# Chunk rows by engine copies, two halves of the first MLP weight, and a new order in a sparse attention and MLP kernel

## The chip, the cores and the metric

The kernel runs on one core of a Trainium2 chip. TensorE (PE in the profile, PEld for its weight loads), VectorE (DVE), ScalarE (ACT) and GpSimd (POOL) work side by side, each through its own list of instructions in order; SyncE (SP) issues most DMAs, GpSimd those that change the type, ScalarE a few. The metric is the device time of one launch in microseconds, lower is better; a time stands as the median of several runs.

## The reference

Attention over 4 batches of 8 heads, 768 positions, 64 columns a head. Keys lie in 24 chunks of 32. Of each chunk the smallest and largest key per column give an upper bound on a query's score; a query sees the six chunks of the highest bound among those that are not in its future. Then follows an MLP with an ELU on the 3072 rows of 512 columns.

```python
k_min = np.min(k_chunks, axis=3)
k_max = np.max(k_chunks, axis=3)
ub = np.sum(np.maximum(q[:, :, :, None, :] * k_min[:, :, None, :, :], q[:, :, :, None, :] * k_max[:, :, None, :, :]), axis=-1)
ub = np.where(causal, ub, -1000000000.0)
top_chunks = np.argsort(ub, axis=-1)[..., -top_k:]
scores = scale * np.matmul(q, k.transpose(0, 1, 3, 2))
...
mask = sel & (pos[:, None] >= pos[None, :])
scores = np.where(mask, scores, -1000000000.0)
...
attn = attn / (np.sum(attn, axis=-1, keepdims=True) + 1e-09)
return np.matmul(attn, v).astype(np.float32)

h = x @ w_in
g = np.where(h > 0.0, h, alpha * (np.exp(np.minimum(h, 0.0)) - 1.0))
return (g @ w_out).astype(np.float32)
```

## The kernel before

The work is cut into eight units of 384 rows. Units 0 and 1 are the first and second 192 positions of batches 0 and 1 (letters `p` and `s` in the names), units 2 to 7 are (batch, half of 384) = (0,1), (1,1), (2,0), (2,1), (3,0), (3,1). Each unit has an attention part and an MLP part, and the MLP of one unit runs on TensorE between the attention of the next.

*Attention.* Keys and queries are transposed (`kT`, `qT`, lines 409 and 549; for batches 2 and 3 by DMA, `kd`, and on VectorE). `kmin` and `kmax` (L373, or `kminc`, `kmaxc`, L492) give the bounds of the chunks, `ub` (L604) their products with the queries, and VectorE transposes them (`ubT`), finds the sixth largest (`max`, L623), marks what lies below (`lt`) and transposes the marks (`sT`). `mk` copies the marks into the tile `rhs`, as 32 rows below the 64 rows of the query (`qa`). The tile `lhs` holds 64 rows of keys (`ka`) and below them 32 *chunk rows*, constants from `econst` that are -40000 where a column belongs to the chunk; so one matmul over 96 rows gives a score with its mask (`sc`, L732 and L786). The chunk rows are written by `chunk_rows` (operations `ec`), for batches 0 and 1 in eight pieces of 32 partitions by 4 x 384 elements. `ex` is the exponential on ScalarE, `tri` the causal mask, `pv` (L758, L837) the product with the values (`v` casts them), `rcp` and `on` (L648, L650) divide, and `px`/`xt` or `xd`, a DMA transpose, turn the result into the tile `xt` for the MLP.

*MLP.* `h{i}.{fc}` (L878) are four matmuls that make 128 of the 2048 inner columns for unit i; `e` (L885, ScalarE) is the exponential, `m` (L887) subtracts one, `g` (L891, VectorE) takes the smaller of `m` and the larger of `h` and 0, into one of 17 `gT` tiles. `o{i}.{tt}.{c}` (L902, for the last tile L856) are four matmuls with the second weight. `oe` copies a finished tile out of PSUM, `out` stores it.

*Weights.* `w_in` is cast by the DMA, from GpSimd's list, in pieces of inner blocks named by `W_IN`; `h` waits for the piece that holds its block. The space of `w_out` serves until then as the place of the first queries and values.

*Order.* Every operation knows on which engines it may run, what it reads and writes and its buffer class. `ORDER` is a string with three characters for each operation: engine and number. It fixes the list of every engine and the order in which all are written out; `PLACES` gives the buffer of each tile. Both were found by a search outside the kernel. `fill` are matmuls on zeros (L941) that write a bank no one reads.

```python
W_IN = ((0, 4), (4, 8), (8, 16))
...
g.op(f"m{i}.{fc}", (POOL, DVE), lambda e, eb=eb, mb=mb: eng[e].tensor_scalar(
    out=ap(mb), in0=ap(eb), scalar1=-1.0, scalar2=1.0, op0=AOT.add, op1=AOT.mult),
    reads=[(eb, 0)], writes=[(mb, 0)])
...
o = g.ops[64 * DIGITS.index(order[j + 1]) + DIGITS.index(order[j + 2])]
o.emit({"P": PE, "A": ACT, "D": DVE, "G": POOL, "S": SP}[order[j]])
```

In the old order GpSimd's list up to the first weight piece is `triz tn1 ident kp ez0 pz tn0 tris2 tris1 sz ka00p0 vz0 es0 ez1 es1 ks0p1 pu oh w_in0`, and the other two pieces follow with two or three short operations between them. TensorE's list around the first MLP blocks is `ub00 fill kT1s1 pxp2 pxp3 fill h0.1 h0.0 h0.3 fill h0.6 h0.4 fill fill h0.2`, five fills, `sc0s01 h0.5 sc0s00 ub10 h0.14`.

Of the kernel before, what the change touches and what calls it, by code (L numbers as in the profile page):

```python
# [45 lines left out]
P1DP3gPjTPjYD1FA2LD27D2GP1VP29D1KPj-P2aP2XD1GP1LPjVD2bP1+D2HP20D2cG2AG2rP33A16A34D2YD1WA1fD21D28
G2ED2ZPk0Pk2P3lGmlG2tG2NG37GmmG2-D22GmnPjXA3hP38P23P2dD3mD3nD24A3jA2uA1MPk4D3oA2ePmuPmqPmCD3pD3q
D3rPjZA2+A30A3iA3cD1gD3tPmOPmGS50AmrPj+S4-D3sGmsAmvPk1DmtA3vPmyD3aAmDG2lAmHA3kPk3Pk6Pk5Pk8A2zPk7
GmwGmID39AmzP3JG3bG1dDmxD35DmJDmAA3KD2SA31PmKDmBGmEAmLP3HP3wD3yPniP41Pm-G2MDmFGmMDmNP3+PmWAmPA42
A3IGmQAm+D3xD2jGmoG3eGmpGn0D3zA40PkaG3uAnjPnmPmSD3AD3LAmTPn2Pn6DmRS4+G43DnkDn1D3BAn7GmUP4FPk9DmV  # L50
A2nDnlAmXP4DD3CPnDG17PnqA4GPnEAn3DmYGn8S4XDn9G3EG3GDmZG3dAnnA4EG3DDnoDnpGn4Dn5A2UP44PnaP4lPneP3S
PnrAnbD2WD36A4mP3QPnsAnfDngS4ZP4MPnFDnhA3RS4YSawA3TDncDndPnwP4OP3NP45P3MG3FG3UP4jPnGD46A4ND4HP4u
PntA4kD47P4ID3OA4PAnHS5wDnuA4vP48P4aP4JP3VS53P3WA49SnvD3PP5ES7LS57G4nD4KP4oD4LP4sP5rP4pP5fA4bD3X
D3YP3ZG4cP4dPnxA5gA4tD4QP4RP4SSblD0nP5QD4wA5hA5sP4eSatP4xP4yD4qA5FD4TA5iP5xD3-SbjD4rD4fA5RPnySaG
D4zD4gP4hD5yP5kD5zA5SScLA5BA5TPnzPkbD4iD4AD5mD4UP4BP58P4VA5tD5lD4CP5JA5GD5aA4WPoxPodAnAPopPnVAoy
D5KD59S51S7SAoeD5LA5NAoqDozG5AG5DG5nG5bDoAG5MP5VA5cSbsGofPnRDorA5oPnZA5qPnJAnWAnSDogGnXDosD5WG54
# [934 lines left out]
```

## Time and profile before

| what | us |
|---|---|
| three runs | 280.07 to 280.51, median 280.38 |
| the profiled execution | 280.4 |
| its span, first to last instruction | 278.7 |
| ScalarE busy | 202.0 |
| GpSimd busy | 153.3 |
| `m` on GpSimd, 104 of them | 54.3 |
| DMA of the chunk rows, eight, issue to landing | median 4.5 each |

In a row of the profile, "out<-in xcount | busy, mean" gives the time that a group of instructions took in all and one of them in ns; what stands behind the second bar is the idle time of the engine ahead of them, and what ended it. A row of a stage gives, behind its bounds, its length and then the busy time and number of instructions of PE, PEld, DVE, ACT and POOL, the granted clock of TensorE, the mean busy share of the DMA engines and GB/s. A row of the waits is "who <- for whom: us in total, times, longest". In the chain and the timeline a row begins with the start and the length in us.

### The profile page before, as it was taken

The page shows a single profiled execution, that of the slowest core. Times are in us where ns is not written, and L with a number is a line of the kernel's source. Part 1 is how long each engine was busy: PE and PEld are TensorE (multiplying, and loading weights), DVE is VectorE, ACT ScalarE, POOL GpSimd, SP SyncE. Part 2 cuts the span into 40 slices and gives each one's busy share as a digit, 9 for nine tenths or more (in the row PEclk, how much of TensorE's full clock was granted, in tenths as well). Part 3 has the DMA queues.
Part 4 walks back from the last instruction along what each step waited for, and adds up shares of the span by engine and source line. Part 5 has one row for each costly group of instructions (what it writes and reads, how often), then busy time and mean ns, then how long its engine had stood idle before and what let it go on. Part 6 is the DMA issues. An engine that isn't in the chain of part 4 may idle for free.

```text
span 278.7 us, 6784 instructions
## 1 busy us (share of the span) xinstructions
PE 260.7 (94%) x2374; PEld 160.8 (58%) x2404; DVE 220.8 (79%) x590; ACT 202.0 (72%) x449; POOL 153.3 (55%) x295
## 2 busy tenths in 40 slices
PE   0798999999999999999999999999999999999995
PEld 0576655585556755565566456665565456665653
DVE  1489998489999999999999997997898766632850
ACT  2066977578898997999599369995898289872621
POOL 6187578212886657878189437763476077300610
PEclk9999999999999999999999999999999999999999
DMA  8999999969959649997499388993900230032002
GB/s 155 214 203 216 212 207 222 202 139 199 199 129 206 146 87 243 210 194 122 121 214 205 69 189 160 184 199 93 224 3 2 58 115 0 2 80 92 1 9 106
DMA packets 118690, 39.25 MB, mean 141 GB/s; under 512 B 111104, under 2 KB 113408, under 8 KB 118656
## 3 DMA queue, kind: packets, MB, share of 16 engines
q1 hardware_dynamic: 112928, 33.67, 59.3%
q0 software_dynamic: 2672, 4.19, 8.2%
q10 hardware_dynamic: 3056, 0.95, 1.7%
q8 instruction: 19, 0.31, 0.5%
q14 instruction: 15, 0.12, 0.2%
HBM read 30.41 MB, written 6.29 MB: 132 GB/s over the span
## 4 chain that ended last, share of the span: by engine, by line
PE 64%; DVE 11%; DMA 10%; issue 5%; ACT 4%; POOL 4%; SPq 1%; DVEq 0%; POOLq 0%; ACTq 0%
PE bank L902 23%; PE bank L878 18%; PE bank L786 8%; PE bank L837 5%; DMA w_in<-in_moe_w_in_dram 5%; DMA f<-in_k_dram 3%; DVE gT L891 3%; POOL m L887 2%; PE bank L409 2%; DMA xt<-on 2%; DVE km L492 2%; PE bank L604 2%; ACT e L885 2%; DVE kst L373 2%; PE bank L758 1%
## 5 line engine op out<-in xcount | busy, mean ns | idle before, releaser
L878 PE MATMUL bank<-xt,w_in 128*128 128x384 bf16 x512 | 92.3, 326 | 0.8 <-DMA w_in<-in_moe_w_in_dram 0.3
L902 PE MATMUL bank<-w_out_sb,gT 128*128 128x512 bf16 x339 | 86.5, 379 | 2.6 <-DVE gT L891 0.7
L887 POOL TENSOR_SCALAR m<-e 128x384 f32<-128x384 f32 x104 | 54.3, 530 | 56.9 <-ACT e L885 51.9
L891 DVE SCALAR_TENSOR_TENSOR gT<-bank,m 128x384 bf16<-128x384 f32 x128 | 66.1, 549 | 15.0 <-POOL m L887 13.5
L801 ACT ACTIVATE pt<-bank 128x384 bf16<-128x384 f32 (+1 forms) x144 | 67.6, 554 | 5.2 <-PE bank L786 4.2
L878 PEld LDWEIGHTS <-w_in 128*128 128x128 bf16 x512 | 49.1, 98 | 34.3 <-issue 2.4
L885 ACT ACTIVATE e<-bank 128x384 f32<-128x384 f32 x128 | 59.4, 496 | 12.3 <-PE bank L878 8.9
L902 PEld LDWEIGHTS <-gT 128*128 128x128 bf16 x368 | 34.3, 97 | 35.2 <-issue 2.5
L786 PE MATMUL bank<-rhs,lhs 96*128 96x384 bf16 (+2 forms) x240 | 44.6, 293 | 0.1
L818 POOL TENSOR_TENSOR pt<-pt,tri 128x256 bf16<-128x256 bf16 (+1 forms) x30 | 26.5, 894 | 10.6 <-ACT pt L801 5.6
L326 ACT ACTIVATE o<-bank 128x512 f32<-128x512 f32 (+1 forms) x18 | 10.6, 590 | 29.5 <-PE bank L902 26.3
L786 PEld LDWEIGHTS <-lhs 96*128 96x128 bf16 x240 | 22.1, 97 | 15.1 <-issue 0.6
L492 DVE TENSOR_REDUCE km<-kc 96x64 f32<-96x1024 f32 x16 | 30.5, 1923 | 0.0
L837 PEld LDWEIGHTS <-pt 128*128 128x128 bf16 x576 | 21.0, 97 | 4.3 <-issue 0.6
L373 DVE TENSOR_REDUCE kst<-bank 128x12 f32<-128x384 f32 x32 | 16.4, 545 | 7.8 <-PE bank L409 7.8
L837 PE MATMUL bank<-vext,pt 128*128 128x65 bf16 x576 | 22.2, 193 | 0.3 <-DVE gT L891 0.3
L328 POOL COPY rhs<-selT 32x384 bf16<-32x384 bf16 (+1 forms) x19 | 12.8, 673 | 14.3 <-DVE selT L632 13.4
L650 DVE TENSOR_TENSOR on<-bank,rcp 128x384 bf16<-128x384 f32 (+1 forms) x40 | 19.7, 495 | 0.6
L328 POOL CAST rhs<-qt 64x384 bf16<-64x384 f32 x33 | 17.5, 540 | 3.1 <-ACT qt L326 1.4
L648 DVE RECIPROCAL rcp<-bank 128x6 f32<-128x6 f32 (+1 forms) x40 | 7.1, 182 | 11.4 <-PE bank L837 7.1
L805 ACT ACTIVATE pt<-bank 128x512 bf16<-128x512 f32 x24 | 14.6, 617 | 0.9 <-PE bank L786 0.8
L328 DVE COPY o<-bank 128x512 f32<-128x512 f32 (+1 forms) x8 | 4.6, 584 | 12.7 <-PE bank L856 6.7
(104 smaller groups left out, 314.0 us busy)
## 6 DMA issues: line engine op xcount, KB each, us to landing
out_dram<-o SPq DMA_DIRECT2D x21, 256.0 KB, 2.4
f<-in_v_dram SPq DMA_DIRECT2D x20, 256.0 KB, 4.4
f<-in_k_dram SPq DMA_DIRECT2D x18, 256.0 KB, 4.7
fx<-in_q_dram SPq DMA_DIRECT2D x32, 96.0 KB, 3.2
kc<-in_k_dram SPq DMA_DIRECT2D x8, 384.0 KB, 4.9
w_out_sb<-in_moe_w_out_dram POOLq DMA_DIRECT2D x4, 512.0 KB, 11.4
f<-in_q_dram SPq DMA_DIRECT2D x6, 256.0 KB, 11.6
w_in<-in_moe_w_in_dram POOLq DMA_DIRECT2D x2, 512.0 KB, 8.6
```

The lines of the kernel that those rows point to most:

```text
L328: eng[e].tensor_copy(out=dst, in_=src)
L373: g.op(("kmin", "kmax")[w] + tag, (DVE,), lambda e, w=w, op=op: nc.vector.tensor_reduce(out=cs(w), in_=src(), axis=AX.X, op=op), reads=[(b ...
L492: nc.vector.tensor_reduce(out=ap(km)[0:96, y, w], in_=ap(kc)[0:96].rearrange("p (w d) -> p d w", d=D), axis=AX.X, op=op), reads=[(kc, 0)], ...
L786: nc.tensor.matmul(ap(banks[hd])[:, o + pc:o + pc + wd], lhsT=apl(ls, G)[0:96, pr, hd, P * kb:P * (kb + 1)], rhs=ap(rs)[0:96, hd, c0 - HS ...
L801: lambda e, hd=hd, pt=pt, banks=banks, wtot=wtot: nc.scalar.activation(out=ap(pt)[:, hd, PAD:PAD + wtot], in_=ap(banks[hd])[:, 0:wtot], fu ...
L818: eng[e].tensor_tensor(out=view, in0=view, in1=tri[:, 64:64 + P].rearrange("p (a b w) -> p a b w", a=1, b=1) .to_broadcast([P, 2, len(dg), ...
L837: nc.tensor.matmul(view()[:, hd, qi, :], lhsT=ap(pt)[:, hd, P * qi + off:P * qi + off + P], rhs=ap(vx[b])[:, kb, 2 * r + hd, :], start=(kb ...
L878: nc.tensor.matmul(ap(bank)[:, 0:HS], lhsT=w_in_sb[x][:, kk, c0:c0 + 2 * P - 1:2], rhs=ap(xT[i, kk]), start=(kk == 0), stop=(kk == NKK - 1))
L885: g.op(f"e{i}.{fc}", (ACT,), lambda e, eb=eb, bank=bank: nc.scalar.activation(out=ap(eb), in_=ap(bank)[:, 0:HS], func=AF.Exp), reads=[(ban ...
L887: g.op(f"m{i}.{fc}", (POOL, DVE), lambda e, eb=eb, mb=mb: eng[e].tensor_scalar(out=ap(mb), in0=ap(eb), scalar1=-1.0, scalar2=1.0, op0=AOT. ...
L891: nc.vector.scalar_tensor_tensor(out=ap(gt), in0=ap(bank)[:, 0:HS], scalar=0.0, in1=ap(mb), op0=AOT.max, op1=AOT.min),
L902: nc.tensor.matmul(ap(bank), lhsT=ap(gts[fc])[:, P * tt:P * (tt + 1)], rhs=w_out_sb[:, fc, :], start=(fc == 0), stop=(fc == NFC - 1))
```

## The change

Four things change. (1) `chunk_rows` is no DMA any more but a copy that VectorE, ScalarE or GpSimd may make; the new order gives three to VectorE, two to ScalarE, three to GpSimd. (2) `W_IN` has two pieces of eight blocks (1024 columns) in place of two of four and one of eight. (3) ScalarE may make `m`, as a copy with a bias of -1. (4) `ORDER` and `PLACES` are new throughout; buffers and their counts are the same. (`on` is only written differently.)

```diff
-W_IN = ((0, 4), (4, 8), (8, 16))
+W_IN = ((0, 8), (8, 16))
...
     def chunk_rows(b, G, half):
         lb = lhs[b]
-        dma(lambda: (apl(lb, G)[er, :, :, HS * half:HS * (half + 1)].rearrange("p a b s -> p (a b) s"),
-                     econst[er, 12 * half:12 * half + 12, :].rearrange("p c w -> p (c w)")
-                     .rearrange("p (a s) -> p a s", a=1).to_broadcast([CHUNK, 4, HS])),
-            [(lb, ("e", half, G))], [(fixed, ("e", half))], f"ec{b}{half}{G}")
+        def emit(e):
+            to = apl(lb, G)[er, :, :, HS * half:HS * (half + 1)].rearrange("p a b s -> p (a b) s")
+            rows = econst[er, 12 * half:12 * half + 12, :].rearrange("p c w -> p (c w)")
+            rows = rows.rearrange("p (a s) -> p a s", a=1).to_broadcast([CHUNK, 4, HS])
+            copy(e, to, rows)
+        g.op(f"ec{b}{half}{G}", (DVE, ACT, POOL), emit, reads=[(fixed, ("e", half))], writes=[(lb, ("e", half, G))])
...
-            g.op(f"m{i}.{fc}", (POOL, DVE), lambda e, eb=eb, mb=mb: eng[e].tensor_scalar(
-                out=ap(mb), in0=ap(eb), scalar1=-1.0, scalar2=1.0, op0=AOT.add, op1=AOT.mult),
-                reads=[(eb, 0)], writes=[(mb, 0)])
+            def less(e, eb=eb, mb=mb):
+                if e == ACT:
+                    nc.scalar.activation(out=ap(mb), in_=ap(eb), func=AF.Copy, bias=-1.0)
+                else:
+                    eng[e].tensor_scalar(out=ap(mb), in0=ap(eb), scalar1=-1.0, scalar2=1.0, op0=AOT.add, op1=AOT.mult)
+            g.op(f"m{i}.{fc}", (POOL, DVE, ACT), less, reads=[(eb, 0)], writes=[(mb, 0)])
```

How many operations of a kind each engine has, where that differs by four or more somewhere:

| operation | before | after |
|---|---|---|
| `m` | GpSimd 104, VectorE 24 | GpSimd 79, VectorE 27, ScalarE 22 |
| `ec` | SP 8 (DMA) | VectorE 3, ScalarE 2, GpSimd 3 |
| `mk` | GpSimd 19, VectorE 7, ScalarE 6 | GpSimd 13, VectorE 12, ScalarE 7 |
| `qr` | ScalarE 20, VectorE 8 | ScalarE 15, VectorE 13 |
| `qa` | GpSimd 33, ScalarE 18, VectorE 5 | GpSimd 31, ScalarE 16, VectorE 9 |
| `v` | GpSimd 13, ScalarE 7, VectorE 6 | GpSimd 13, ScalarE 11, VectorE 2 |
| `fill` | 40, of them 24 ahead of the first `h` | 40, of them 34 ahead of the first `h` |

In the new order GpSimd's list begins `tnz tn0 sz idz ident kz kq tn1 ez1 pu es0 v1p1 ks1p0 ka10p1 ka00p1 tris2 pz oh v0p0 es1 w_in0 ks0s1 ks0p0 ks0s0 w_in1`; VectorE's begins `zeros kp kmin0p0 ez0 ka00p0 identb kmax1p0 triz kmin1p0`. TensorE begins with two fills, `qT0p1 kT0p1 kT0p0`, and has around the first blocks `ub00`, two fills, `pxp2 kT1s1`, seven fills, `pxp3`, three fills, `h0.0 h0.1 h0.3 h0.4 fill h0.5 sc0s11 h0.2 ub10 h0.6 h0.8`. `v0p0` waits for the fifteenth load in SP's list.

More of the change, by code (lines that the diff above doesn't have):

```diff
@@ L46 @@
[L46 to L56, printed above, removed]
-Po5S7OD5XSbBDnYD5ZD5YPnNA5CAn-A5vPo1PkdPolG5PGnTAnKDnUAnOSbmS55SnIGnLDnMG0hD5-PohAo6Po9A5dGn+GnP
@@ L649, in divide, with scaled @@
              reads=[(o3, 0), (o3, 1)], writes=[(rcp, 0)])
[L650 to L653 removed]
+        def scaled(e):
+            nc.vector.tensor_tensor(
+                out=ap(on)[:, 0:nt].rearrange("p q h d -> p h q d"), in0=view()[:, :, :, 0:D],
+                in1=ap(rcp)[:, :, 0:nt].to_broadcast([P, 2, nt, D]), op=AOT.mult)
+        g.op("on" + tag, (DVE,), scaled, reads=[(o3, 0), (o3, 1), (rcp, 0)], writes=[(on, 0)])
         return on
```

146 lines of the change are left out of this document (77 added, 69 removed).

## The prediction

> **What bounds the kernel now.** I read the page's first section and the stage table first: is one engine full, and where not? The stages are cut where TensorE begins the MLP of the next unit.
>
> ```profile
> span 278.7 us, 6784 instructions
> PE 260.7 (94%) x2374; PEld 160.8 (58%) x2404; DVE 220.8 (79%) x590; ACT 202.0 (72%) x449; POOL 153.3 (55%) x295
> ...
> core 0: us, PE busy (x) PEld busy (x) DVE busy (x) ACT busy (x) POOL busy (x), PEclk, DMA share, GB/s
> 8.00:20.00 12.00, 10.94 (x80) 8.12 (x81) 9.38 (x20) 4.22 (x9) 6.23 (x25) 1.00 1.37 207
> 20.00:30.00 10.00, 8.62 (x146) 6.67 (x143) 8.37 (x30) 7.22 (x16) 7.97 (x22) 1.00 1.27 216
> 30.00:38.10 8.10, 7.68 (x77) 4.48 (x74) 7.67 (x30) 7.65 (x18) 4.07 (x10) 1.00 1.14 210
> 65.00:101.30 36.30, 35.87 (x337) 22.18 (x339) 34.70 (x84) 33.11 (x76) 23.57 (x43) 1.00 0.78 167
> 101.30:137.10 35.80, 34.51 (x347) 20.34 (x349) 33.95 (x98) 31.28 (x73) 25.39 (x43) 1.00 0.84 176
> 162.10:195.20 33.10, 32.73 (x286) 19.85 (x290) 28.70 (x50) 27.78 (x64) 20.03 (x35) 1.00 0.81 163
> 195.20:222.50 27.30, 26.62 (x243) 15.12 (x245) 24.30 (x84) 20.00 (x43) 13.37 (x22) 1.00 0.31 73
> ```
>
> In the stages shown from 65 us on TensorE is busy for 96 to 99% of the time, at the full granted clock. VectorE stands at 96% (34.70 of 36.30) and 95% (33.95 of 35.80) in the two stages to 137 us. Whether that fullness costs TensorE anything is told by its waits, here those from 38 us to the end:
>
> ```profile
> PE bank L902 <- DVE gT L891: 0.7, 2, 0.4
> PE bank L503 <- DVE rcp L648: 0.6, 1, 0.6
> PE bank L902 <- issue: 0.5, 3, 0.2
> PE bank L878 <- DMA w_in<-in_moe_w_in_dram: 0.3, 1, 0.3
> PE bank L878 <- DMA xt<-on: 0.3, 1, 0.3
> PE bank L837 <- DVE gT L891: 0.3, 1, 0.3
> ```
>
> The sum is 2.7 us in 240: a new order can win hardly more than that behind 38 us, and every us that TensorE starts late at 38 us is a us at the end. So the head decides. There I read the chain of waits, and the timeline of TensorE and GpSimd:
>
> ```profile
> 10.01 2.02 PE bank L409 x11
> ...
> 24.59 13.48 DMA w_in<-in_moe_w_in_dram
> ...
> 17.10 3.86 POOL L290 MEMSET onehot<- 32x1 bf16 x24
> 20.90 0.99 POOL L296 DMA_DIRECT2D w_in<-in_moe_w_in_dram  x1
> 22.80 0.82 POOL L296 DMA_DIRECT2D w_in<-in_moe_w_in_dram  x1
> 24.59 0.80 POOL L296 DMA_DIRECT2D w_in<-in_moe_w_in_dram  x1
> ...
> 29.48 0.61 PE L673 MATMUL bank<-ident_b,on 128*128 128x128 bf16 x8
> 30.10 2.19 PE L878 MATMUL bank<-xt,w_in 128*128 128x384 bf16 x12
> 32.24 1.46 PE L878 MATMUL bank<-xt,w_in 128*128 128x384 bf16 x8
> 34.41 0.97 PE L941 MATMUL bank<-zeros 128*128 128x256 bf16 x5
> 38.12 0.82 PE L878 MATMUL bank<-xt,w_in 128*128 128x384 bf16 x4 [0.33 <-DMA w_in<-in_moe_w_in_dram]
> ...
> DMA to landing us min/median/max: 7.8/9.4/13.5
> ```
>
> The last row belongs to the three w_in transfers. Taken in their order, they land at 20.90 + 7.8 = 28.7, 22.80 + 9.4 = 32.2 and 24.59 + 13.5 = 38.1 us; the last two are the starts at 32.24 and 38.12. The first MLP matmul, at 30.10, waits for the attention of unit 0 (L673, ended at 30.09), not for its weights. Between 30.1 and 38.1 TensorE has seven `h` blocks, two scores and `ub10`, and fills the rest with matmuls on zeros.
>
> **The change, part by part.**
>
> *Weights in two halves.* 1024 columns now arrive as one piece, so the first usable weights land when both quarter pieces landed before, 32.2 - 20.9 = 11.3 us behind the first issue at most, and the second half 38.1 - 32.2 = 5.9 us later. Until then TensorE has in the new order seven `h` blocks, one score, `ub10` and a fill ahead of `h0.8`, the first on the second half. The three blocks at 30.10 take 2.19 with the drain of the last matmul, so a block is some 0.66 us and seven are 4.6. From the last fill's start (34.41 + 0.97 less one fill of 0.27, so 35.1) to the wait of 0.33 ahead of 38.12 there are 2.7 us, which hold one block, two scores and `ub10`; so 1.7 of the 6.3 us stand for `ub10`, a score and the fill. That is about as long as the gap between the halves (5.9): neither side waits long, and the later first half costs nothing while the second half sets the end of this stretch.
>
> The Trainium skill, "DMA: Bandwidth & Descriptors", section "Anatomy of one DMA — SWDGE (gpsimd) path", speaks for fewer pieces: some 2.0 us fixed and 436 GB/s behind it for each DMA. Three pieces into two would by it save an estimated 2.0 us; the trace says that the pieces overlap (issues 1.9 us apart, landings 3.5 and 5.9 apart), so I count none of it.
>
> *When is the first half issued?* GpSimd's list up to it is new. `es0` waits on VectorE's `ez0`, behind `kmin0p0`, behind `kT0p0` on TensorE, behind two of ScalarE's key loads. The like wait before ended at 10.01; the first load is now 96 KB instead of 192, so between 9.0 and 10.0 here, and `es0` starts at 10.2 to 11.2 (0.4 for the transposes, 0.6 for `kmin`, 0.2 for `ez0`). Then these rows:
>
> ```profile
> L281 POOL TENSOR_SCALAR_AFFINE_SELECT econst<-econst 32x384 bf16<-32x384 bf16 x2 | 1.2, 616 | 0.1
> L339 POOL TENSOR_SCALAR vext<-f 128x512 bf16<-128x512 f32 x11 | 7.4, 669 | 0.1
> L328 POOL COPY lhs<-kt x5: 496/501/566, 12.8 to 46.5; 64x384 bf16<-64x384 bf16 x5
> L252 POOL MEMSET pt<- 128x1024 bf16 x2 | 1.9, 952 | 0.1
> ```
>
> `es0` 0.62, `v1p1` 0.67, some 0.9 for `ks1p0` and the wait on `kmin1p0`, two key copies 1.0, `tris2` 0.25, `pz` 0.95, `oh` 0.27 + 3.86, `v0p0` 0.67, `es1` 0.62: 9.8 us, so the issue falls at 20.0 to 21.0 against 20.90. I take 20.3, 0.6 earlier. Both ends are kept.
>
> *Chunk rows off the DMA.* Eight copies of 96 KB go; by the order of SP's queue three of them stood among the loads ahead of the weights.
>
> ```profile
> lhs<-econst SPq DMA_DIRECT2D x8, 96.0 KB, 4.5
> ...
> L328 POOL COPY rhs<-selT 32x768 bf16<-32x768 bf16 x9 | 7.8, 865 | 6.4 <-DVE selT L632 6.0
> L326 ACT ACTIVATE rhs<-selT 32x768 bf16<-32x768 bf16 x3 | 2.5, 841 | 0.1
> L328 DVE COPY rhs<-selT 32x768 bf16<-32x768 bf16 x4 | 1.7, 427 | 0.1
> ```
>
> At the 207 GB/s of the stage to 20 us, 3 x 98 KB are 1.4 us of transfer, which clears the loads out of the way of an earlier weight issue (that is why I let the 0.6 through whole). In exchange come 32x1536 copies, not in the trace: bounded by twice the row of 768 from above and once from below, 0.43 to 0.85 us on VectorE (three), 0.84 to 1.68 on ScalarE (two), 0.87 to 1.73 on GpSimd (three). I take the upper ends. ScalarE's two and one of VectorE's stand in the head: VectorE's work up to the last normalisation (`on1p3`) grows by some 0.6 us by counting the operations ahead of it, up to `xtp2` by 1.6. The first block then starts 0.6 to 1.6 behind the 30.10 of before; plus 6.3 is 37.0 to 38.0 for `h0.8`, against 38.12. So attention allows a gain of 0.1 to 1.1, with the 0.6 in its middle.
>
> The Trainium skill, "SBUF — State Buffer", section "SBUF: two separate sides", speaks against: a VectorE copy in a two-port mode locks GpSimd out for its whole length. In this trace the five key copies of GpSimd up to 60 us lie between 496 and 566 ns, 0.07 us apart, while VectorE was 78 to 95% busy in the stages to 38 us; so no such lock-out shows. By the rule the chunk copy `ec100` on VectorE, ahead of the weight issue, would take an estimated 0.85 us from the 0.6 and leave nothing; that is in the rival "same" below.
>
> *ScalarE subtracts one.* 22 of 128 `m` go to ScalarE, 27 to VectorE (24 before), 79 to GpSimd (104).
>
> ```profile
> L887 POOL TENSOR_SCALAR m<-e 128x384 f32<-128x384 f32 x104 | 54.3, 530 | 56.9 <-ACT e L885 51.9 <-DVE gT L891 1.6 <-DVE kt L328 0.7
> L887 DVE TENSOR_SCALAR m<-e 128x384 f32<-128x384 f32 x24 | 12.0, 503 | 1.0 <-ACT e L885 0.7
> L885 ACT ACTIVATE e<-bank 128x384 f32<-128x384 f32 x128 | 59.4, 496 | 12.3 <-PE bank L878 8.9 <-POOL m L887 1.2 <-POOL rhs L328 0.6
> ```
>
> An `m` on ScalarE is not in the trace; from the `e` row it is 0.46 us (59.4/128) to 0.50, so 10 to 11 us more there and 13 less on GpSimd. ScalarE's fullest stage, 65 to 101 us, has 36.30 - 33.11 = 3.2 us free and gets two of them, with other work leaving. It hides everywhere; uncovered it would be 0.5 us for each.
>
> *The order.* All the rest is a new sequence. TensorE's work is the same, 40 fills in both; ahead of the first block stand 34 of them instead of 24, and behind the start of the second half five instead of eight. At (0.97 - 0.27) / 4, some 0.17 us each, that is 0.5 saved, less 0.2 for the one score that is left behind. On the other side, VectorE's list between 162 and 195 us grows, by count of its operations, by one reduction of `kc` and, net, six others (a block of maxima, two transposes of `ubT`, three casts of `qa` and more; two masks less).
>
> ```profile
> L492 DVE TENSOR_REDUCE km<-kc 96x64 f32<-96x1024 f32 x16 | 30.5, 1923 | 0.0
> ```
>
> With the others at 0.4 to 0.5 us, as the `m` row has, that is 1.9 + 2.7 = 4.6 us, where 33.10 - 28.70 = 4.4 were free. The new order's own waits are unknown: between minus 2.7 (all that there are) and plus 4.6 (VectorE's growth with no cover). I take 0: from 65 to 137 us VectorE was 95% full, and TensorE's waits for it from 38 us on add up to 1.6 us.
>
> *The end.* Before, two VectorE pieces of the last tile close it, now one ScalarE piece of 256 columns; both are 0.4 to 0.5 us, 0.
>
> **Sum**, on the profiled execution's 280.4 us (span 278.7, 1.7 around it; the median is 280.38): -0.6 head, -0.3 fills less the score, 0 for the rest, about 279.5.
>
> **The rivals.**
> 1. *Same: the weights come when they came.* Late key loads (`es0` at 11.2) or a lock-out put the issue at 20.9 again; fills and waits cancel: 280.2. For it: both ends of the issue time lie that near. Against: the queue is shorter.
> 2. *Slower: VectorE becomes the bound from 162 to 195 us.* 28.7 + 4.6 = 33.3 us of work in a stage of 33.1. `gT` then runs late into L902. What VectorE keeps of its 4.4 idle adds to the 0.2 that are over, and from 0.7 kept on it eats the gain of 0.9. Two thirds kept, 2.9, give 280.4 - 0.9 + 3.1 = 282.6. For it: the row. Against: part of that work comes out of the next stage (3.0 free), and stages 95% full were borne.
> 3. *Slower: the first half comes late.* GpSimd's `v0p0` stands ahead of the weight issue and waits for the fifteenth load of SP. Some 3.1 MB of loads end with it, 15 us at 207 GB/s; with 1 us ahead and 2 to land I estimate 18. GpSimd is ready for it at 20.3 - 1.3 = 19.0, and from there every us is paid: landed at 20.9, the issue is 22.2, the end 280.4 + 1.3 - 0.3 = 281.4.
> 4. *Faster by more:* the waits behind 38 us go too, 1.5 of 2.7: 278.0.
>
> **How the numbers follow.** Within 0.2% (0.56 us) is what a measurement of this kernel cannot tell from no change. The forecast of 279.5 gets 0.32, rival 4 gets 0.14: faster 0.46. Rival 1 gets 0.15. Rival 2 gets 0.19, rival 3 gets 0.10, and other waits of the new order 0.10 (281 to 284): slower 0.39. Likeliest's own range 278.9 to 280.1 (issue at 20.0 to 21.0). Low end 277.2: the head at its best (-1.1), fills (-0.3) and two thirds of the 2.7. High end 283.4: past rival 2 (282.6) and most of the other waits, short of 284.1, rival 2 with all 4.4 kept.
>
> **What would show it.** Right: the first w_in issue at 20.0 to 20.6, `h0.8` at 37.2 to 37.8 and ended by the weights, VectorE under 34.7 and 33.9 in the stages to 137 us, TensorE's waits behind 38 us at 2 to 4 us. Wrong: an issue past 21 us, GpSimd waiting on a v load, an `h0.0` held by `xtp2` past 32 us, L902 waiting on gT between 160 and 200 us, or waits of more than 5 us in all.

## The result, and the profile after

The changed kernel takes 283.92 us (median of 4 runs, 283.27 to 284.63) against 280.44 (4 runs, 280.07 to 281.03) beside it: ratio 1.0123, 95% interval 1.0089 to 1.0156, so slower, and by more than the 0.2% that the prediction set as its limit. In a second group it took 283.47 against 280.32. The forecast was 279.5, with a range up to 283.4.

Below are the page's first section and stages of the profile after, cut as before at the starts of an MLP. Line numbers are some lines higher now: the first MLP matmuls are L881 (were L878), `m` L894 and on ScalarE L892 (L887), `g` L897 (L891), the second MLP matmuls L908 (L902), fills L947 (L941), the mask multiplications `tri` L821.

```profile
span 282.5 us, 6805 instructions
PE 265.3 (94%) x2404; PEld 161.9 (57%) x2404; DVE 228.0 (81%) x602; ACT 213.0 (75%) x472; POOL 144.7 (51%) x267
...
8.00:20.00 12.00, 9.27 (x45) 6.04 (x45) 8.38 (x18) 4.30 (x6) 6.58 (x23) 1.00 1.33 201
20.00:30.00 10.00, 9.86 (x156) 7.63 (x155) 9.08 (x28) 9.44 (x20) 6.42 (x21) 1.00 1.25 202
30.00:39.00 9.00, 8.24 (x104) 5.29 (x89) 8.60 (x33) 8.55 (x20) 5.08 (x10) 1.00 1.14 210
65.80:101.70 35.90, 35.65 (x339) 22.04 (x338) 33.39 (x80) 33.20 (x77) 22.43 (x39) 1.00 0.80 161
101.70:137.60 35.90, 34.68 (x351) 20.28 (x350) 33.34 (x98) 32.20 (x75) 26.68 (x47) 1.00 0.91 183
163.80:197.50 33.70, 33.23 (x291) 19.72 (x289) 29.05 (x51) 29.10 (x68) 18.03 (x30) 1.00 0.67 142
197.50:226.80 29.30, 28.11 (x251) 15.45 (x249) 27.00 (x92) 20.43 (x45) 11.35 (x18) 1.00 0.30 70
```

VectorE is not fuller where rival 2 put the loss: 29.05 of 33.70 us from 163.8 to 197.5, with 51 instructions where there were 50; the rival needed it full. Its growth is in the next stage: 27.00 of 29.30 us, 92%, where it was 24.30 of 27.30. That stage is 2.0 us longer, but the one behind it is 1.8 shorter (31.3 us, 33.1 before), so the stages alone don't place the loss. TensorE's waits behind 38 us:

```profile
PE bank L840 <- DVE pt L821: 0.8, 1, 0.8
PE bank L505 <- DVE rcp L650: 0.8, 1, 0.8
PE bank L881 <- DVE gT L897: 0.6, 2, 0.5
PE bank L881 <- DMA xt<-on: 0.6, 2, 0.4
PE bank L789 <- DVE gT L897: 0.6, 2, 0.4
PE bank L840 <- POOL pt L821: 0.5, 1, 0.5
PE bank L908 <- DVE gT L897: 0.4, 2, 0.3
```

They add up to 4.3 us where there were 2.7, and two of them are new in kind: `pv` waits for causal masks (`pt` from L821). To see where TensorE falls behind I laid its matmuls in list order beside each other in the two traces, without the fills, and took the time at which the same amount of work was done, in the kernel before and in the other. The rows are worked out so from the traces; a plus is behind the kernel before.

| kernel, profiled run | 31.6 us | 46.5 | 72.0 | 113.8 | 155.8 | 206.5 | 257.4 |
|---|---|---|---|---|---|---|---|
| changed | +3.1 | +1.0 | +0.8 | +0.1 | +1.9 | +2.8 | +3.8 |
| changed, second profile | +2.2 | +0.6 | +0.5 | -0.1 | +1.3 | +1.6 | +2.6 |
| `g1_head` | +0.4 | -1.0 | -1.1 | -1.8 | -0.2 | +0.5 | +1.5 |
| `g2_late_before` | +2.7 | +0.6 | +0.5 | +1.3 | +1.5 | +1.5 | +1.5 |
| `g4_late_after` | -0.1 | +0.3 | +0.3 | +0.1 | +1.0 | +1.2 | +3.7 |
| `h1_seam` | +0.4 | -1.0 | -1.2 | -1.3 | -1.1 | -1.1 | -1.0 |

So the new order starts the MLP 3 us late, has 2 of them back at 46 us (ten fills fewer are left for later), wins the rest up to 114 us, and loses 2.7 to 3.7 us behind that. There are two losses, then: one in the head, one behind 114 us. The head, in the timelines of GpSimd, VectorE, ScalarE and TensorE and the landings of the two weight pieces:

```profile
11.97 0.61 POOL L281 TENSOR_SCALAR_AFFINE_SELECT econst<-econst 32x384 bf16<-32x384 bf16 x1 [6.51 <-DVE econst L252]
...
15.24 1.28 POOL L268 TENSOR_SCALAR_AFFINE_SELECT tri<-tri 128x64 bf16<-128x64 bf16 x1
...
22.51 0.99 POOL L296 DMA_DIRECT2D w_in<-in_moe_w_in_dram  x1
26.05 0.38 POOL L378 TENSOR_TENSOR kst<-kst 128x12 f32<-128x12 f32 x2 [2.55 <-DVE kst L375]
...
27.06 0.79 POOL L296 DMA_DIRECT2D w_in<-in_moe_w_in_dram  x1
...
15.11 1.32 DVE L328 CAST vext<-w_out_sb 64x512 bf16<-64x512 f32 x1
...
32.31 0.35 DVE L328 COPY xt<-bank 128x384 bf16<-128x384 bf16 x1
32.64 0.47 ACT L326 ACTIVATE xt<-bank 128x384 bf16<-128x384 bf16 x1
...
17.40 0.61 PE L699 MATMUL bank<-xt,kt 64*128 64x64 bf16 x8 [0.95 <-DVE xt L328]
33.23 2.39 PEld L881 LDWEIGHTS <-w_in 128*128 128x128 bf16 x16 [1.03 <-DMA w_in<-in_moe_w_in_dram]
33.24 2.77 PE L881 MATMUL bank<-xt,w_in 128*128 128x384 bf16 x16 [0.76 <-DVE thr L625]
...
DMA to landing us min/median/max: 10.7/11.3/11.9
```

`es0` (first row) starts at 11.97, having waited for VectorE's `ez0`. Then `tris2` takes 1.28 us beside VectorE's cast `v0p1` of 1.32. The first weight half is issued at 22.51 and lands 10.7 later, at 33.2; the second waits behind `ks` operations for VectorE, is issued at 27.06 and lands at 39.0. TensorE's first `h` starts at 33.24, when its weight load has waited 1.03 us for the first half. The matmul's own row names VectorE's `thr`, but the maximum that ends at that moment (`max000`) stands behind `xtp2` in VectorE's list, and `h0.0` does not read it. The last two copies of attention are done at 32.66 (`xtp2`, on VectorE) and 33.11 (`xtp3`, on ScalarE). So weights and attention came at nearly the same moment, both three us late. In the second profile everything is somewhat sooner: `es0` at 11.24, the first half issued at 21.77, the first `h` at 32.16.

### The profile page after: what moved, and what is told of

Its sections match the earlier page's. It is cut to its first block, busy times and chain, and to the rows that moved or that the text cites. A ratio compares the mean times of both kernels' runs of the same rounds, so it can differ in the third digit from the quotient of the medians.

```text
span 282.5 us, 6805 instructions
## 1 busy us (share of the span) xinstructions
PE 265.3 (94%) x2404; PEld 161.9 (57%) x2404; DVE 228.0 (81%) x602; ACT 213.0 (75%) x472; POOL 144.7 (51%) x267
## 3 DMA queue, kind: packets, MB, share of 16 engines
q1 hardware_dynamic: 112304, 33.11, 58.1%
## 4 chain that ended last, share of the span: by engine, by line
PE 55%; DVE 24%; ACT 7%; DMA 7%; POOL 3%; issue 3%; SPq 0%; DVEq 0%; POOLq 0%; ACTq 0%
PE bank L908 23%; PE bank L881 8%; DVE gT L897 7%; PE bank L789 7%; PE bank L840 6%; DMA f<-in_k_dram 3%; DVE km L494 3%; ACT e L888 3%; DVE kst L375 2%; DMA fx<-in_q_dram 2%; DVE thr L625 2%; PE bank L606 2%; PE bank L551 2%; POOL m L894 1%; DVE m L894 1%
## 5 line engine op out<-in xcount | busy, mean ns | idle before, releaser
L881 PE MATMUL bank<-xt,w_in 128*128 128x384 bf16 x512 | 92.0, 326 | 2.0 <-DVE thr L625 0.8
L908 PE MATMUL bank<-w_out_sb,gT 128*128 128x512 bf16 x368 | 90.3, 379 | 0.5 <-DVE gT L897 0.4
L897 DVE SCALAR_TENSOR_TENSOR gT<-bank,m 128x384 bf16<-128x384 f32 x128 | 65.6, 547 | 9.6 <-POOL m L894 6.5
L804 ACT ACTIVATE pt<-bank 128x384 bf16<-128x384 f32 (+1 forms) x144 | 68.6, 564 | 5.7 <-PE bank L789 4.0
L881 PEld LDWEIGHTS <-w_in 128*128 128x128 bf16 x512 | 49.2, 98 | 36.1 <-issue 4.1
L894 POOL TENSOR_SCALAR m<-e 128x384 f32<-128x384 f32 x79 | 41.3, 532 | 55.8 <-ACT e L888 47.2
L908 PEld LDWEIGHTS <-gT 128*128 128x128 bf16 x368 | 34.3, 97 | 34.9 <-issue 1.7
L821 POOL TENSOR_TENSOR pt<-pt,tri 128x512 bf16<-128x512 bf16 (+1 forms) x32 | 30.3, 954 | 21.1 <-ACT pt L804 19.6
L326 ACT ACTIVATE o<-bank 128x512 f32<-128x512 f32 (+1 forms) x16 | 9.3, 583 | 20.1 <-PE bank L908 18.9
L840 PE MATMUL bank<-vext,pt 128*128 128x65 bf16 x576 | 22.4, 193 | 1.2 <-DVE pt L821 0.8
L328 POOL CAST rhs<-qt 64x384 bf16<-64x384 f32 x31 | 15.7, 510 | 3.1 <-ACT qt L326 2.1
L894 DVE TENSOR_SCALAR m<-e 128x384 f32<-128x384 f32 x27 | 12.9, 489 | 4.0 <-ACT e L888 3.5
L328 POOL COPY rhs<-selT 32x768 bf16<-32x768 bf16 (+1 forms) x13 | 9.4, 720 | 10.2 <-DVE selT L634 9.6
L328 DVE COPY o<-bank 128x512 f32<-128x512 f32 (+1 forms) x10 | 5.9, 600 | 10.3 <-PE bank L908 5.2
```

Source lines behind the costliest of these rows:

```text
L328: eng[e].tensor_copy(out=dst, in_=src)
L804: lambda e, hd=hd, pt=pt, banks=banks, wtot=wtot: nc.scalar.activation(out=ap(pt)[:, hd, PAD:PAD + wtot], in_=ap(banks[hd])[:, 0:wtot], fu ...
L821: eng[e].tensor_tensor(out=view, in0=view, in1=tri[:, 64:64 + P].rearrange("p (a b w) -> p a b w", a=1, b=1) .to_broadcast([P, 2, len(dg), ...
L840: nc.tensor.matmul(view()[:, hd, qi, :], lhsT=ap(pt)[:, hd, P * qi + off:P * qi + off + P], rhs=ap(vx[b])[:, kb, 2 * r + hd, :], start=(kb ...
L881: nc.tensor.matmul(ap(bank)[:, 0:HS], lhsT=w_in_sb[x][:, kk, c0:c0 + 2 * P - 1:2], rhs=ap(xT[i, kk]), start=(kk == 0), stop=(kk == NKK - 1))
L894: eng[e].tensor_scalar(out=ap(mb), in0=ap(eb), scalar1=-1.0, scalar2=1.0, op0=AOT.add, op1=AOT.mult)
```

## The experiments

In each part the time of the kernel before comes from the same chip; "over" is the difference of the medians. The changed kernel is 3.5 over, in its second group 3.15.

### One part taken out of the changed kernel

Theories at this point: M, ScalarE's `m` delay its other work; V, VectorE is too full from 138 to 227 us; R, the copies of chunk rows make the head late; W, the first weight piece is too large; O, the new sequence itself costs.

```diff
 e1_m_back: m of 22 blocks
-ScalarE
+GpSimd
 e2_vector_light: 36 of qr, qa, mk, m, tri, oe from unit 3's first h to unit 7's
-VectorE
+the engine that has them in the kernel before
 e3_rows_dma: chunk_rows as before, the first four behind the load of v1s1
-g.op(f"ec{b}{half}{G}", (DVE, ACT, POOL), emit, ...)
+dma(lambda: ..., f"ec{b}{half}{G}")
 e4_three: the two quarters issued back to back
-W_IN = ((0, 8), (8, 16))
+W_IN = ((0, 4), (4, 8), (8, 16))
```

> The changed kernel with ScalarE's 22 subtractions given to GpSimd, all else as it is. If ScalarE's subtractions delay its exponentials and so TensorE (theory M), the growth of the lag behind 137 us (3.4 us) goes: 280.5 to 281.5. If the sequence and VectorE's load there are the cause (theories O and V), it stays within 0.7 us of 283.9, or grows, since GpSimd gets 11.5 us more.

287.88 us, 6.9 over the kernel before (1.0247, 1.0217 to 1.0276). M falls: in the new order GpSimd can't take the 22 operations back.

> The changed kernel, with 36 operations that VectorE got from ScalarE or GpSimd between the first MLP block of unit 3 and that of unit 7 (qr, qa, mk, m, tri, oe) given back to the engine that had them before, in their place in the order. Theory V (VectorE too full from 138 to 227 us): TensorE's lag behind 137 us shrinks by 2 us or more, 281 to 282. Theory O (the sequence itself): within 0.7 us of 283.9. Theory M: no better, ScalarE gets 12 operations more: 284 to 285.

286.5, 5.5 over (1.0193, 1.0169 to 1.0217), outside all three ranges. With 36 operations fewer on VectorE the time grew, so V falls. GpSimd got 25 of them and ScalarE 11, and what they lose by it can't be told apart here.

> The changed kernel with the chunk rows by DMA again, the first four behind the last of the loads in SP's list, the other four where the copies stood. If the copies cost VectorE and ScalarE time in the head (0.7 and 3.0 us there), h0.0 comes up to 1 us earlier; but the weights set the stretch (issued 22.5 and 27.1), so theory O expects 283.5 to 284.2. If the copies are what made the head late (theory R): 282.9 or less.

283.21, 2.25 over (1.0091, 1.0065 to 1.0118), between the ranges of R and O, and its interval overlaps that of the changed kernel. In its trace the lag at 46 us is 0.5, where the two profiles of the changed kernel have 1.0 and 0.6, and behind 114 us it grows as before. At most some 1 us of the loss is R's, in the head, and even that isn't shown.

> The changed kernel with the first weight in three pieces, the two quarters issued one behind the other where the first half stood. Theory W (the larger first piece makes the head late): h0.0 starts before 32 us and the end is 0.7 us or more earlier, 283.2 or less. Theory O: h0.0 is held by xtp2 and the second half by its issue at 27.1, so nothing: 283.6 to 284.2.

283.61, 2.65 over (1.0094, 1.0062 to 1.0126), inside the interval of the changed kernel. The first `h` starts at 31.86 us, before 32 as W had it, but then TensorE waits 1.03 us for the second half, to 39.48; the end is not where W put it. W isn't shown.

### One part put into the kernel before

```diff
 e5_before_halves
-W_IN = ((0, 4), (4, 8), (8, 16))
+W_IN = ((0, 8), (8, 16))
 e6_before_rows: the eight ec at their old places in the order
-SP, by DMA
+the engines of the changed kernel
 e7_before_m: the same 22 m, at their old places
-GpSimd, VectorE
+ScalarE
```

> The kernel before with the weight in two halves, issued where its first and its third piece stood (20.9 and 24.6). Theory W (the larger first piece costs): h blocks start at 32.2 instead of 30.1 and 0.5 to 2 us are paid at the end. My prediction's step says nothing is paid, since the second half still lands at about 38: 280.2 to 280.8.

281.96, 1.1 over (1.0045, 1.0028 to 1.0062).

> The kernel before with the chunk rows copied by the engines that the changed kernel uses (three VectorE, two ScalarE, three GpSimd), at the same places of the order. Theory R (the copies cost): 0.5 to 2 us more, above all if ScalarE's or GpSimd's 1.5 us copies hold up the head. Theory O: within 0.5 us of 280.4.

283.09, 2.3 over (1.0101, 1.0062 to 1.0139).

> The kernel before with the same 22 subtractions on ScalarE as in the changed kernel. Theory M (ScalarE's subtractions cost): 281.5 or more. Theory O: within 0.5 us of 280.4.

285.88, 5.1 over (1.0188, 1.016 to 1.0216).

Each part alone makes the old order slower, 8.5 us in sum, while the changed kernel with all three is 3.5 slower. (A part of this is the granted clock of the last section: it was halved for a stretch in all four runs of `e6` and in two of `e7`, which took 1.2 us longer than its other two.) In the new order the first two are worth at most some 1 us each, and the third gains 3.4. That fits an order which was found for its parts: a part tried in an order that was made without it tells more of that order than of the part. So I cut the order instead.

### The order cut in two

In the changed kernel the cut is at `h2.4`, about 110 us, where it stands level with the kernel before. Behind it come the list and the engines of the other kernel, with 112 operations on another engine (111 in `g4_late_after`); the tiles there get the buffer that has been free longest.

```diff
 g1_head, GpSimd (ez0 was VectorE's):
-... tn1 ez1 pu es0 v1p1 ks1p0 ka10p1 ka00p1 tris2 pz oh v0p0 es1 w_in0 ks0s1 ks0p0 ks0s0 w_in1
+... tn1 ez1 ez0 es0 pu pz es1 v1p1 ks1p0 ka10p1 ka00p1 tris2 oh v0p0 w_in0 w_in1 ks0s1 ks0p0 ks0s0
 g1_head, VectorE:
-max001 kmin1s0 xtp2
+xtp2 max001 kmin1s0
 g2_late_before: the changed kernel up to h2.4
-the changed order behind it
+the order before
 g3_head_late: both
 g4_late_after: the kernel before up to h2.4
-the order before behind it
+the changed order, 14 m on ScalarE among it
```

> The changed kernel with its head mended and nothing behind it touched. On GpSimd the constants ez0, es0, pz and es1 go ahead of its copy of v1p1 (ez0 on GpSimd instead of VectorE), and the second half of the weight is issued directly behind the first; on VectorE the transpose copy xtp2 goes ahead of max001. Theory H (the head's loss is the late issue of the two halves, 22.51 and 27.06 us): first half issued at 20.5 to 21.3 us, second 1 us behind it, first h at 31.0 to 32.3 instead of 33.24 us, no TensorE wait of over 0.3 us for the second half, and the end 0.7 to 1.2 us sooner than the changed kernel: 282.7 to 283.2 us against 280.8 of the kernel before. Rival (what the head loses is taken back between 46 and 110 us anyway, as the changed kernel's own lag falls from +0.9 to 0 there): the end moves by under 0.3 us, 283.6 to 284.2.

282.23, 1.30 over (1.004, 1.002 to 1.006): 1.9 to 2.2 less than the changed kernel, more than I expected, and with an earlier issue than I expected. Its timelines of GpSimd and TensorE:

```profile
19.22 1.75 POOL L296 DMA_DIRECT2D w_in<-in_moe_w_in_dram  x2
...
30.61 2.76 PE L881 MATMUL bank<-xt,w_in 128*128 128x384 bf16 x16 [0.22 <-DVE ubT L623]
```

Both halves are issued from 19.22 on, and the first `h` is 2.6 us sooner than in the changed kernel. The lead stays: of 2.7 us at 31.6 us (first table) 2.3 are left at the end. The rival that it is taken back anyway falls.

> The changed kernel up to h2.4 on TensorE (about 110 us of its profiled execution, where its work stands level with the kernel before), and from there the order and the engines of the kernel before, with the tiles behind the cut put in the free buffer that has been free longest. The chunk rows and the two halves stay, since they all lie ahead of the cut. Theory O (the new order behind 110 us loses the time): 280.2 to 281.2 us. Rival P (the late loss comes from parts that stay: rows, halves, what the head leaves behind): 283 to 284.5 us.

282.02, 1.09 over (1.004, 1.0023 to 1.0056). O has most of the loss behind 110 us, though 0.8 us of what I expected did not come.

> Both edits at once: the head mended as in the first kernel of this group and the order of the kernel before from h2.4 on. Theories O and H together: 279.3 to 280.3 us, the fastest so far; if only O holds 280.2 to 281.2; if neither, 283 or more.

281.17, 0.24 over (1.0005, 0.9986 to 1.0024): no difference left to the kernel before that can be told, but 0.9 above the upper end expected of both.

> The mirror of the second kernel of this group: the kernel before up to h2.4 (weight in three pieces, chunk rows by DMA), and from there the order and engines of the changed kernel, 14 subtractions on ScalarE among them. Theory O: the loss comes along with the late order alone, 283.5 to 284.8 us. Rival P: 280.6 to 281.5 us, as the kernel before.

283.09, 2.16 over (1.0083, 1.0056 to 1.011). The late order alone brings the loss along, 0.4 us less of it than I expected.

What `g2` and `g3` fell short by is at the seam; from `g3_head_late`'s timeline of TensorE:

```profile
112.44 0.81 PE L881 MATMUL bank<-xt,w_in 128*128 128x384 bf16 x4 [1.03 <-DVE gT L897]
...
114.73 1.02 PE L908 MATMUL bank<-w_out_sb,gT 128*128 128x512 bf16 x4 [0.45 <-DVE gT L897]
```

Two waits, 1.5 us together, for `g` tiles whose `m` stand in GpSimd's list behind copies that the first order had left over.

### Single waits

Is the late loss a handful of waits, each worth its length (S), or is the order short of engine time everywhere (D)?

```diff
 h2_tri, from g1_head: the masks tri2000 and tri3010
-GpSimd
+VectorE
 h1_seam, from g3_head_late: m2.4 and m2.11
-GpSimd
+ScalarE
 h1_seam, GpSimd's copies qa0201 and ky200
-ahead of m2.1 and m2.13
+behind m2.14
```

> The changed kernel with its head mended (282.23 us), and two causal-mask multiplications moved from GpSimd to VectorE: tri2000 and tri3010, those that ran beside a VectorE instruction just ahead of TensorE's waits of 0.47 us at 149.2 and 0.78 us at 214.1 us (a mask of 0.29 us took 1.18 us there on VectorE, ending with GpSimd's). Theory S (the late loss is a handful of single waits, each worth its length): both waits under 0.15 us, and the end 0.7 to 1.2 us sooner, 281.0 to 281.5. Rival D (the order behind 110 us is short everywhere, and a wait taken away comes back at the next tile): the end moves by less than 0.4 us, 281.8 to 282.6.

281.25, 0.57 over (1.0012, 0.9989 to 1.0035): 0.7 us less over than `g1_head`, with intervals that overlap (1.0 us by the medians alone, which come from two chips). Laid beside the kernel before as in the table, it falls back by 1.2 us between 46 and 257 us, `g1_head` by 2.4. TensorE, VectorE and GpSimd in `g1_head` first:

```profile
214.08 0.47 PE L840 MATMUL bank<-vext,pt 128*128 128x65 bf16 x10 [0.78 <-DVE pt L821]
...
212.84 1.18 DVE L821 TENSOR_TENSOR pt<-pt,tri 128x256 bf16<-128x256 bf16 x1
...
212.72 1.15 POOL L821 TENSOR_TENSOR pt<-pt,tri 128x512 bf16<-128x512 bf16 x1 [0.21 <-ACT pt L804]
```

And in `h2_tri`, TensorE and VectorE:

```profile
213.29 0.57 PE L840 MATMUL bank<-vext,pt 128*128 128x65 bf16 x12
...
213.06 0.27 DVE L821 TENSOR_TENSOR pt<-pt,tri 128x256 bf16<-128x256 bf16 x1
...
213.98 0.41 DVE L821 TENSOR_TENSOR pt<-pt,tri 128x512 bf16<-128x512 bf16 x1
```

In the first, GpSimd's mask runs from 212.72 to 213.87 and VectorE's from 212.84 to 214.02: the shorter one, 0.27 alone, lasts until GpSimd's has ended, and TensorE waits 0.78 us for it. In the second both run on VectorE, in 0.27 and 0.41 us, and the wait is gone, as is the one at 149 us. (There it was GpSimd's mask that TensorE waited for: four masks took GpSimd from 146.61 to 150.36 us, beside two `m` on VectorE that took 1.80 us together.) At 214 us, moving work *to* the fuller engine made both masks faster.

> The kernel with mended head and the late order of the kernel before (281.17 us), with only its seam at 112 us mended: m2.4 and m2.11 stay on ScalarE as in the changed kernel, and the GpSimd copies qa0201 and ky200 go behind its last subtraction of that unit, m2.14. Its profile had TensorE waits of 1.03 and 0.45 us there for VectorE's g. Theory S: 1.0 to 1.6 us sooner, 279.6 to 280.3 us, below the kernel before (280.9). Rival D: under 0.4 us, 280.8 to 281.4.

279.80, 0.88 below the kernel before (0.9963, 0.9943 to 0.9984), 1.1 below `g3_head_late` by these differences. It is the fastest kernel here: the mended head and the middle of the new order, the late part of the old. S holds in `h1_seam`, where the waits taken away came out at the end. In `h2_tri` both waits are gone and the end lies where S put it, but the difference is not clear of the noise.

### What the head lost

Two causes are possible in the head: the weights (W, here their late issue), or TensorE's clock (C). The timelines show the clock in the length of a fill, first after, then before:

```profile
20.74 0.61 PE L947 MATMUL bank<-zeros 128*128 128x256 bf16 x2
...
23.01 0.38 PE L947 MATMUL bank<-zeros 128*128 128x256 bf16 x2
```

```profile
14.17 0.63 PE L941 MATMUL bank<-zeros 128*128 128x256 bf16 x2
...
17.11 0.38 PE L941 MATMUL bank<-zeros 128*128 128x256 bf16 x2
```

Two fills take 0.61 or 0.63 us while the clock is low and 0.38 later on. By the trace's first clock record the full clock comes at 22.4 us in the changed kernel, at 16.0 in the kernel before, at 14.6 in `g1_head`. (Ahead of that record a stage shows 1.00 all the same.)

```diff
 i0_changed_again: the changed kernel
 i1_mask_apart, GpSimd:
-tris2 pz oh v0p0 es1 w_in0
+pz oh tris2 v0p0 es1 w_in0
 i2_weights_only, GpSimd (xtp2 ahead of max001 on VectorE):
-tris2 pz oh v0p0 es1 w_in0 ks0s1 ks0p0 ks0s0 w_in1
+tris2 es1 v0p0 w_in0 w_in1 pz oh ks0s1 ks0p0 ks0s0
 j1_weights_late, from g1_head, GpSimd:
-tris2 oh v0p0 w_in0 w_in1 ks0s1 ks0p0 ks0s0
+tris2 v0p0 oh w_in0 ks0s1 ks0p0 ks0s0 w_in1
 j2_weights_early, from i2_weights_only, GpSimd: pz
-behind w_in1
+behind pu
```

> The changed kernel once more, as the measure for the next two on the same chip. Expected 283.3 to 284.6 us; TensorE's clock granted in full only at 21 to 22.5 us of the span, as in its first profile (22.3; the kernel before 16.0, the kernel with the mended head 14.6).

283.47, 3.15 over (1.0102, 1.0084 to 1.012), full clock at 22.6 us.

> The changed kernel with one GpSimd instruction moved: the mask constant tris2 goes behind pz and oh, away from VectorE's cast v0p1, with which it ran side by side (1.28 and 1.32 us; alone 0.25 to 0.41 and 0.46). Theory C (the head's loss comes from the granted clock: the long cast makes TensorE wait 0.95 us for xt at 17.4 us, and without a stretch of 3.4 us of full work the full clock comes at 22.3 us instead of 14 to 18): cast under 0.6 us, full clock by 19 us, first h 1.0 to 2 us sooner than 33.24 although the first weight issue comes only 0.9 sooner (21.4 to 21.7), second half awaited for more than 0.3 us, and the end 0.8 to 1.5 us below the changed kernel. Theory W (the loss is the late weights): the end 0.4 to 0.8 us below, by the 0.9 of the issue that go with it, and no more.

283.92, 3.6 over (1.0125, 1.0105 to 1.0145). The edit missed its aim: the cast now ran beside `pz` and the start of `oh`, and took as long. The full clock came at 14.0 us, but was halved again from 17.4 to 20.8.

```profile
14.78 1.52 DVE L328 CAST vext<-w_out_sb 64x512 bf16<-64x512 f32 x1
...
32.33 2.78 PE L881 MATMUL bank<-xt,w_in 128*128 128x384 bf16 x16 [0.17 <-DMA w_in<-in_moe_w_in_dram]
```

The first `h` waits for the weights, as in the changed kernel; the end is not sooner, and neither theory's range is met.

> The changed kernel with its weights early and tris2 left beside the cast: es1 and v0p0 go directly behind tris2 on GpSimd, both weight halves directly behind v0p0, the constants pz and oh behind them; xtp2 goes ahead of max001 on VectorE. Issues at 19.2 to 20.0 and 20.2 to 21.0 us, as in the kernel with the mended head. Theory W: first h at 31.0 to 31.6, the end 1.3 to 1.9 us below the changed kernel. Theory C: full clock again at 21 to 22.5 us, first h held by attention at 32.0 to 33.2 us, the end 0.2 to 0.9 us below the changed kernel.

283.62, 3.3 over (1.0112, 1.009 to 1.0134). Here the cast was short (0.45 us) and the full clock came at 18.9 us, but attention was late for another reason, the constant `pz`:

```profile
23.48 0.20 PE L761 MATMUL bank<-vext,pt 128*128 128x65 bf16 x1 [1.36 <-POOL pt L252]
...
33.20 2.76 PE L881 MATMUL bank<-xt,w_in 128*128 128x384 bf16 x16 [0.21 <-DVE ubT L623]
```

Weights issued from 20.7 us on, and the first `h` at 33.20 again, now held by attention. An earlier full clock and earlier weights gained nothing here, and the end lies in neither theory's range.

> The kernel with the mended head (282.23 us), all of it kept but the weights: the constant oh goes behind v0p0 and ahead of the first half (issue about 23.0 us instead of 19.2), and the second half goes behind ks0s0 as in the changed kernel (about 25.3). Theory W (with attention in time, the late halves alone cost what the head lost): TensorE's first h at 33.4 to 34.0 us instead of 30.61, waiting for the weights, and the end 283.2 to 284.3. Theory C (clock and attention, not the weights): the end 282.0 to 282.7.

283.22 (282.23 to 286.06), 2.7 over (1.0091, 1.0054 to 1.0128): with the late weights 1.4 us of the mended head's 1.9 to 2.2 are lost again (by the two intervals, 0.2 to 2.6). By W's lowest bound just a hit. The profiled run is one of the longer ones (285.35):

```profile
33.16 4.46 PE L881 MATMUL bank<-xt,w_in 128*128 128x384 bf16 x16 [2.89 <-DMA w_in<-in_moe_w_in_dram]
...
30.52:33.94 3.42, 0.78 (x5) 0.51 (x6) 3.38 (x11) 1.32 (x4) 3.02 (x4) 1.00 1.12 204
33.94:37.35 3.41, 3.41 (x13) 1.62 (x11) 1.93 (x5) 1.77 (x4) 0.69 (x2) 0.52 1.13 206
```

TensorE is through with attention at 30.3 us (33.16 less 2.89) and waits for the first half; behind this wait the clock is halved for 3.4 us (0.52), so the first four blocks take 4.46 us instead of 2.76. Two of the eight runs had this (mean clock 0.992 and 0.994). The other six have a median of 282.70, which is 0.9 us more over than `g1_head`; that much is the wait itself.

> The kernel i2_weights_only with one mishap mended: the constant pz, for which TensorE waited 1.36 us at 23.5 us there, goes to where the kernel with the mended head has it, behind pu. Weights issued at 19.2 to 20.8 us. Theory M (the first h starts at the later of weights and attention, so that both had to come forward): no wait for pz, first h at 31.0 to 32.0, the end 282.0 to 282.8, as with the mended head. Theory C: 283.2 to 284 as before, unless the full clock comes before 18 us here.

282.65, 2.1 over (1.0076, 1.0052 to 1.0099), 1.2 below `i2_weights_only`: with the wait for `pz` gone, the first `h` starts at 30.76, a little sooner than M said. It starts at the later of weights and attention, and both had to come forward (M).

What the late clock costs by itself stays open: `i1` was meant to tell it and didn't.

## Why the prediction was wrong

*TensorE sets the end: right.* Its work is the same, and waits that were taken away (`h1_seam`, less clearly `h2_tri`) or put in (`j1_weights_late`) came out at the end.

*"So the head decides", since the waits behind 38 us are 2.7 us: wrong.* They bound what an order can win there, not what it can lose. By `g2_late_before` the late order cost 2.1 to 2.4 us, by `g4_late_after` 2.2. With the 1.9 to 2.2 of the head that is more than the 3.15 to 3.5 measured, as the new order wins about 1 us between (with both losses mended, `h1_seam` ends 0.9 below the kernel before).

*The first half's issue, 20.3 us in the sum: the first step that failed.* It was 22.51, in the second profile 21.77: past the 21 us that I had named as a sign of being wrong. `es0` started at 11.97 (11.24) and not at 10.2 to 11.2. The key loads were not late: TensorE's wait for them ended at 9.91 (9.18), inside the 9.0 to 10.0 that I gave. But from there to `es0` I counted 1.2 us, and it took 2.06: 0.74 for the transposes, 0.56 for the reduction, 0.38 for `ez0`, and gaps of 0.12 to 0.13 between. From `es0` to the issue I had 9.8 us; it took 10.5, of which `tris2` has 1.0 too much, being 1.28 in place of the 0.24 to 0.28 that it takes in the kernel before. The second half was not costed at all: I let it follow the landing of the first by 5.9 us, which it did (39.0 less 33.2 is 5.8), by luck: GpSimd waited 2.55 us for `kst` ahead of its issue. The load of its first weights, for `h0.8`, then began at 38.98, where I had 37.2 to 37.8 for the block. In place of a gain of 0.6 the head lost 1.9 to 2.2 us by `g1_head`; late weights alone lost 1.4 by `j1_weights_late`.

*Attention in time, a gain of 0.1 to 1.1: wrong by about 1.5 to 2.5 us.* I bounded the first block at 30.7 to 31.7; it was 33.24, with `xtp3` copied at 33.11. VectorE's list was counted in durations alone, without the cast of 1.32 us and without the 0.95 that TensorE then waits for `xt`, at the low clock.

*Halves cost nothing: open in the changed kernel, wrong in the old order.* `e4_three` is inside the interval of the changed kernel, where the wait for the second half is 0.15 us, at the weight load. In the old order (`e5_before_halves`) the step said 280.2 to 280.8, and the halves cost 1.1 us; there the first `h` waited for the first half until 32.44.

*Chunk rows and `m`: the sizes were right.* From the views of the two lines:

```profile
L328 DVE COPY lhs<-econst x3: 551/552/1059, 19.3 to 88.9; 32x1536 bf16<-32x1536 bf16 x3
L328 POOL COPY lhs<-econst x3: 1457/1460/1541, 32.8 to 60.4; 32x1536 bf16<-32x1536 bf16 x3
L326 ACT ACTIVATE lhs<-econst x2: 1478/1478/1479, 12.6 to 19.0; 32x1536 bf16<-32x1536 bf16 x2
L892 ACT ACTIVATE m<-e x22: 506/524/593, 34.6 to 270.9; 128x384 f32<-128x384 f32 x22
```

All copies but one lie inside their bounds (0.43 to 0.85 on VectorE, one of 1.06; 0.84 to 1.68; 0.87 to 1.73), and `m` on ScalarE takes 0.52 where I had 0.46 to 0.50. That they hide there is not shown by itself: they cost less than on GpSimd (`e1_m_back`), and in the old order they cost 5.1 us (`e7_before_m`).

*"I take 0" for the new order's own waits, between -2.7 and +4.6: the second step that failed.* The listed waits grew by 1.6 us. The reason I gave for the upper end, VectorE full between 162 and 195 us, is not it: rival 2 falls by the stages (86% busy there, 92% in the next) and by `e2_vector_light`. What the runs show in its place are single waits for single tiles, two of them (1.25 us) for masks that ran while GpSimd and VectorE were both at work. The listed waits are not all of the 2.1 to 2.4 us that the late order cost; where the rest goes stays open.

*"No such lock-out shows": wrong.* I went by one kind of GpSimd copy. The Trainium skill, "SBUF — State Buffer", section "SBUF: two separate sides", says that whichever starts first of a GpSimd instruction and a VectorE one with two SBUF inputs holds a port pair that they share for its whole length. The two masks at 212.7 us agree: 1.15 us on GpSimd, and VectorE's 0.27 until that has ended. The trace of the kernel before had it too: its 24 `m` on VectorE take 0.32 to 1.17 us, median 0.36, and the longest, 210.34 to 211.50 us, ends just behind a mask on GpSimd that ends at 211.29. I had weighed the rule in the head alone and for the copy `ec100`, beside which GpSimd's `oh` lost nothing (its 24 small pieces took 3.54 us, 3.86 in the kernel before).

Rival 3, the first half late (issue at 22.2, the end at 281.4), had the right effect with the wrong cause: `v0p0` did not wait for its load.

## What to carry to other kernels

An engine that is 96% busy has little to win and much to lose: a new order is to be costed upward from zero, tile by tile, at the few places where the full engine waits on one producer, and not by the fullness of stages. A start that needs two chains comes with the later one, so trace both to the first instruction; and mending one of them alone may show nothing. Parts that came with a new order can't be judged one at a time: cut the order at a point where both kernels stand level, and exchange one side.
